# A new order for the written list of attention and early routing steps in a fused attention and expert kernel

## The chip, the cores and the metric

The kernel runs on one core of a Trainium2 chip. The metric is device time in microseconds (us). The engines are named as in the profile: PE (TensorE), DVE (VectorE), ACT (ScalarE), POOL (GpSimd), and SP (SyncE), which issues most DMAs.

## The reference

```
x = attention(q, k, v)             # 2 batches, 8 heads, 576 tokens, head_dim 64, window of 64 tokens
x = x as [1152 tokens, 512]
x = moe(x): expert = argmax(x @ w_gate), gate = softmax at it, at most cap = 288 tokens per expert
            out[token] = gate * (relu(x[token] @ w1[expert]) @ w2[expert])     # 8 experts, 512 -> 1024 -> 512
out = (g @ w_out), h = x @ w_in, g = h * clip(h + 3, 0, 6) / 6                # 512 -> 2048 -> 512
```

## The kernel before

**Stages.** Attention works on nine tiles of 128 tokens (index j) and on 18 halves of heads (index g, two for each j). The routing of the first five tiles ("early routing") runs inside attention's tail: it picks the expert with the most tokens among them, gathers up to 128 of that expert's rows from DRAM, and runs that expert on them with weights loaded ahead ("early loads", eight of 512 KB into the tile `early`). Then come the other experts and the dense layer. Their order is set by a planner with costs and due times that starts from the state in which attention ends.

**The list.** Attention and early routing are not planned at build time. They are written as one list of words, `ATTENTION` (L317), which `run_nodes` (L434) walks: each word is a step, a number behind the point is its tile or half, and `:a` or `:v` puts a copy on ACT or DVE. Every engine takes its own steps in the list's order and waits by semaphores for what a step needs, so the list is an order for each engine and not a timetable between them. The words that matter here:

- `lq lk lv`: loads of 256 KB of q, k, v by SP; `st.j`: store of tile j's attention output to `x_dram`, also by SP.
- `tq tk tv`, `pt`, `tw`: transposes on PE; `eq ek ev`, `ep`, `ew`, `ex`: the copies of these out of PSUM, on ACT or DVE (`ep.16` is a copy into the tile pT, `ex.8` two copies into vx and vy); `cv0 cv1 cv2`: copies of v on POOL.
- `s.j`: scores on PE (L574); `m.g`: mask and maximum on DVE (L587, four scans and their sums); `e.g`: exponentials on ACT (L600); `av.j`: values on PE (L628); `f.j`: division and logits on DVE (L640).
- `top pl fl gE ie`: early routing on DVE (L130 to L795); `pl` writes the expert's number to `eI` (L746), `ie` writes the row numbers and `sgE`, the gates. `pp`, `ix`: its counts and indices on PE. `hotp`: products for the later routing on POOL (L892).
- `wl.u.h`: an early load by SP (L271 for w1, L274 for w2); it needs `eI`. `ga`: the gather of the early expert's rows from `x_dram` into the tile c, issued by POOL (L800); it needs `ie` and the stores of tiles 0 to 4.
- `sE`: scaling of the gathered rows by their gates on ACT (L468); `tE`: their transposes on PE (L815); `xE`: copy of these into `early` on ACT; `e0.u` to `e3.u`, `er`, `et`, `eh`: the early expert on its first three units.
- `ch cn pL rk sa px sx g0 ...`: the routing of all tiles, up to the first gather for the other experts, into `first_w`.

**PSUM banks.** `gw`, `tw`, `pp`, `ix` and `tE` share one bank, the tag "x" (L100), so `tE` can be written only when the copies `ex.8` of `tw.8` have been read out of it.

**SP.** All DMAs of SP go out in order. A store that waits for its tile holds back every load behind it. The DMAs of SP and those of POOL are different queues on the same DMA engines.

```
node("ga", {"P": 0.4}, early_gather, ["ie"], lag=6.0)
node("sE", {"A": 0.61, "V": 0.5}, early_scale, ["ga"])
node(("wl", u, h), {"D": 1.46}, early_load(u, h), ["pl"], lag=2.3)
```

Of the kernel before, what the change touches and what calls it, by code (L numbers as in the profile page):

```python
# [23 lines left out]
def tile_kernel(ctx, tc, q, k, v, w_gate, w1, w2, w_in, w_out, out, cap):  # L24
# [87 lines left out]
    ex = const.tile(T3, F32, name="ex")  # L112
# [175 lines left out]
    def big(name, dt=F32):  # L288
        return rt.tile([128, NJ, E], dt, name=name)

    def sq(name):
# [7 lines left out]
    p1, bT, rk = logits, ex, big("rk")  # L299
    sa = rt.tile([128, NJ], F32, name="sa")  # L300
# [14 lines left out]

    NWARM = 9
    ATTENTION = """  # L317
        lq.0 tq.0 lk.0 tk.0 lk.1 eq.0:a lq.1 lq.2 ek.0:a tk.1 s.0 lv.0 m.0 tq.1 ek.1:a tq.2 eq.1:a m.1 e.0 wg tv.0
        s.1 eq.2:v pt.0 ev.0:v e.1 ep.0:a gw.0 ew.0:a lk.2 m.3 m.2 tk.2 pt.1 ek.2:a ep.1:v rc tw.0 lv.1 lq.3 lk.3
        cv1.0 tv.1 e.2 s.2 pt.2 ev.1:a lv.2 lk.4 tq.3 ex.0:v cv1.1 cv2.1 cv0.1 e.3 tk.3 eq.3:a cv0.0 ek.3:a av.0 m.5  # L320
        m.4 f.0 gw.1 ep.2:a s.3 e.4 m.7 cv2.0 ew.1:a pt.3 lq.4 ep.3:a tw.1 ex.1:v m.6 tv.2 tk.4 ev.2:a e.5 lv.3 pt.4
        ek.4:a ep.4:v tq.4 eq.4:v cv0.2 av.1 gw.2 f.1 e.6 lv.4 s.4 e.7 pt.6 cv0.3 tv.4 ew.2:v tv.3 cv1.2 tw.2 cv2.3
        ep.6:v lq.5 pt.5 ev.4:a lk.5 tk.5 ev.3:a cv2.2 cv1.3 ep.5:a tq.5 pt.7 ex.2:v ek.5:a eq.5:a av.2 gw.3 lq.8
        lk.6 m.8 m.9 ep.7:v cv1.4 s.5 cv0.4 tk.6 cv2.4 e.9 ew.3:a f.2 m.11 tw.3 lq.6 lv.6 lq.7 tq.6 e.8 ex.3:a pt.9
        gw.4 m.10 st.0 eq.6:a ep.9:v ew.4:v av.3 tw.4 cv0.6 pt.8 e.11 ek.6:a lv.5 lk.7 s.6 ex.4:a cv0.5 f.3 ep.8:a
        av.4 e.10 tk.7 tv.6 cv2.5 m.12 ek.7:a pt.10 ev.6:a tq.7 ep.10:a f.4 top gw.6 cv1.5 tq.8 m.13 ew.6:a eq.7:a
        lv.8 pp tv.5 eq.8:a cv2.6 ev.5:a pt.11 lk.8 cv1.6 lv.7 e.13 s.7 pl gw.5 st.4 tv.8 fl st.2 cv0.7 st.3 ew.5:a
        ep.11:a st.1 tw.5 gE ex.5:a pt.13 cv1.7 tw.6 av.5 e.12 ex.6:a m.14 tv.7 ix ev.8:a ep.13:a ev.7:a tk.8 ie
        ek.8:a cv0.8 pt.12 wl.2.1 gw.7 ep.12:a wl.3.1 ew.7:a m.15 f.5 wl.0.0 tw.7 cv1.8 wl.2.0 s.8 wl.1.0 e.15 pt.15
        e.14 ga hotp.3 ep.15:a wl.1.1 hotp.0 st.5 wl.0.1 wl.3.0 ex.7:v m.17 e.17 av.6 m.16 gw.8 pt.14 ew.8:a f.6  # L330
        pt.17 ep.14:a tw.8 av.7 e.16 ep.17:v pt.16 ex.8:a f.7 sE:a ep.16:a tE st.7 st.6 xE:a cv2.7 av.8 f.8 e0.1 ch
        e1.1 e0.0 pL er.1:v hotp.1 hotp.2 hotp.4 cn rk e1.0 sa hot.6 et.1 er.0:a et.0 eh.1:a e0.2 hot.8 hot.7 eh.0:a
        e2.0 px e1.2 sx e3.0 gt g0 hot.5 e2.1 gc pg e3.1 er.2:v sg
    """
    with ExitStack() as actx:
        ac = actx.enter_context(tc.tile_pool(name="ac", bufs=1))
# [379 lines left out]
        e1 = [ac.tile([128, 1], F32, name=f"e1_{i}") for i in range(2)]  # L716
        et = [ac.tile([128, NE], F32, name=f"et_{i}") for i in range(5)]
# [332 lines left out]
    for n, (small, b) in enumerate(TEAMS):  # L1050
        at_ = dict.fromkeys("abw", 0)
        order = ORDER[n]
        for c in order:
            f = at_[c]
# [867 lines left out]
    for g, (small, b) in enumerate(TEAMS):  # L1922
        st = start[False, small[0]]
# [81 lines left out]
    for n, (rest, u) in enumerate(own):  # L2005
        r = own_hidden(rest, u, r_up)
        if rest and u < 3:
            s, i, _ = rows_at[u]
# [83 lines left out]
```

## Time and profile before

| | |
|---|---|
| median of 3 runs | 412.59 us (412.42 to 412.99) |
| the profiled execution | 413.24 us |
| its span, first to last instruction | 411.5 us |
| mean granted TensorE clock | 0.994 |
| PE busy | 398.0 us (97%) |
| DVE, ACT, POOL busy | 277.5, 236.0, 49.7 us |
| moved by DMA | 65.43 MB, mean 159 GB/s |

Times in the rows count from the span's first instruction. A row of a timeline is the start, the duration, the engine, the line of the kernel, the operation, and what it writes and reads; in square brackets stands how long the engine was idle before it and what ended that. PE's matmuls overlap, so its busy time is not the same as its peak. SP's DMA issues are short; the transfers behind them are not.

### The profile page before, as it was taken

What the parts mean: (1) busy time and instruction counts of PE and PEld (TensorE: products, weight loads), DVE (VectorE), ACT (ScalarE), POOL (GpSimd) and SP (SyncE); (2) the same over time, 40 slices, a digit from 0 to 9 for tenths busy, and PEclk for the clock granted to TensorE, in tenths of its full rate; (3) what the DMA queues carried; (4) which work ended last, traced back from release to release, by engine and by line L of the source; (5) the groups of instructions that cost most, each with busy time, mean ns of one, the idle gap of its engine ahead of it and who ended that gap; (6) DMA issues with size and microseconds to landing.
All of it is one profiled execution on the core that took longest, in us unless ns stands there. A gap on an engine that the chain in (4) does not pass through costs nothing.

```text
span 411.5 us, 8431 instructions
## 1 busy us (share of the span) xinstructions
PE 398.0 (97%) x3066; PEld 341.2 (83%) x3066; DVE 277.5 (67%) x772; ACT 236.0 (57%) x519; POOL 49.7 (12%) x109
## 2 busy tenths in 40 slices
PE   8999989999999999999999999999999999999992
PEld 4888676669998999798899898888888888989981
DVE  1898956898789789866798999368794222222530
ACT  3898961876776566657877575466672223232320
POOL 8443414040011000000000000000000000200211
PEclk9999999999999999999999999999999999999997
DMA  9996986996687989999500740041500000100101
GB/s 171 207 211 156 300 305 203 364 299 210 214 283 248 358 278 298 312 353 308 211 2 0 245 165 2 1 133 73 205 1 2 0 0 2 76 27 0 51 30 56
DMA packets 63842, 65.43 MB, mean 159 GB/s; under 512 B 30688, under 2 KB 47072, under 8 KB 63792
## 3 DMA queue, kind: packets, MB, share of 16 engines
q1 hardware_dynamic: 62224, 59.79, 46.8%
q0 software_dynamic: 1568, 5.01, 3.7%
q8 instruction: 26, 0.43, 0.4%
q14 instruction: 24, 0.20, 0.1%
HBM read 60.08 MB, written 4.72 MB: 157 GB/s over the span
## 4 chain that ended last, share of the span: by engine, by line
PE 89%; DMA 3%; DVE 3%; ACT 2%; issue 1%; POOL 0%; POOLq 0%; ACTq 0%; DVEq 0%
PE banks L244 75%; PE banks L510 2%; DMA c<-x_dram,eI 2%; PE banks L574 2%; PE banks L628 2%; PE banks L610 1%; PE banks L1473 1%; PE banks L667 1%; PE banks L1498 1%; DMA out_dram<-part,cidx 1%; PE banks L1308 1%; PE banks L1557 1%; DMA x_dram<-xt 1%; PE banks L1406 0%; PE banks L540 0%
## 5 line engine op out<-in xcount | busy, mean ns | idle before, releaser
L244 PE MATMUL banks<-x,wt 128*128 128x320 f32 (+3 forms) x432 | 79.8, 336 | 0.0
L244 PEld LDWEIGHTS banks<-x,wt 128*128 128x128 f32 x432 | 70.8, 188 | 7.1
L244 PE MATMUL banks<-wt,g 128*128 128x512 f32 x288 | 69.6, 390 | 0.0
L263 DVE TENSOR_TENSOR wt<-raw,wt 128x512 fp32r<-128x512 f32 x100 | 64.5, 686 | 4.6 <-ACT wt L258 4.3
L1619 DVE SCALAR_TENSOR_TENSOR gf<-r,banks 128x320 f32<-128x320 f32 (+3 forms) x48 | 26.5, 553 | 60.2 <-ACT r L1616 60.1
L1616 ACT ACTIVATE r<-banks,c_three 128x320 f32<-128x320 f32 (+3 forms) x48 | 27.9, 582 | 68.3 <-PE banks L244 68.1
L244 PEld LDWEIGHTS banks<-wt,g 128*128 128x128 f32 x288 | 53.7, 188 | 10.6
L258 ACT CAST wt<-raw 128x512 fp32r<-128x512 f32 x100 | 58.9, 630 | 4.6 <-PE banks L244 4.0
L244 PE MATMUL banks<-xT,wt 128*128 128x224 f32 (+2 forms) x288 | 38.2, 282 | 0.0
L244 PE MATMUL banks<-h,wt 128*128 128x224 f32 (+2 forms) x288 | 37.0, 279 | 0.0
L244 PEld LDWEIGHTS banks<-xT,wt 128*128 128x128 f32 x288 | 34.8, 191 | 1.6 <-issue 0.4
L244 PEld LDWEIGHTS banks<-h,wt 128*128 128x128 f32 x288 | 34.6, 192 | 0.8 <-issue 0.8
L1622 ACT CAST g<-gf 128x320 fp32r<-128x320 f32 (+2 forms) x40 | 21.4, 534 | 16.5 <-DVE gf L1619 16.4
L1625 DVE TENSOR_TENSOR g<-gf,g 128x320 fp32r<-128x320 f32 (+2 forms) x40 | 23.4, 584 | 10.1 <-ACT g L1622 9.4
L1662 POOL DMA_INDIRECT out_dram<-raw,cidx x4 | 3.9, 983 | 203.9 <-ACT raw L1659 196.4
L244 PE MATMUL banks<-x,wt_fixed 128*128 128x320 f32 (+3 forms) x144 | 26.8, 337 | 0.4 <-ACT x L1389 0.4
L244 PEld LDWEIGHTS banks<-x,wt_fixed 128*128 128x128 f32 x144 | 23.5, 188 | 3.0 <-ACT x L1389 0.7
L206 ACT ACTIVATE c<-raw 128x512 f32<-128x512 f32 x32 | 21.6, 674 | 6.2 <-DVE raw L229 4.6
L244 PE MATMUL banks<-wt_fixed,g 128*128 128x512 f32 x96 | 23.2, 390 | 0.0
L600 ACT ACTIVATE pe<-neg,nmx 128x128 f32<-128x128 f32 x72 | 22.7, 400 | 0.0
L222 DVE SCALAR_TENSOR_TENSOR c<-raw,c 128x512 uint32<-128x512 uint32 x32 | 22.1, 690 | 0.7
L587 DVE CUSTOM_DVE_ANT_0 neg<-banks,tmask 128x128 f32<-128x128 f32 x72 | 16.1, 286 | 8.5 <-PE banks L574 8.3
(310 smaller groups left out, 627.5 us busy)
## 6 DMA issues: line engine op xcount, KB each, us to landing
raw<-in_moe_w_dram SPq DMA_DIRECT2D x56, 512.0 KB, 5.3
raw<-in_moe_w_in_dram SPq DMA_DIRECT2D x16, 512.0 KB, 6.0
raw<-in_moe_w_out_dram SPq DMA_DIRECT2D x16, 512.0 KB, 6.1
early<-in_moe_w_dram SPq DMA_DIRECT2D x8, 512.0 KB, 7.2
x_dram<-xt SPq DMA_DIRECT2D x9, 256.0 KB, 5.1
q_sb<-in_q_dram SPq DMA_DIRECT2D x8, 256.0 KB, 4.9
k_sb<-in_k_dram SPq DMA_DIRECT2D x8, 256.0 KB, 4.6
v_sb<-in_v_dram SPq DMA_DIRECT2D x8, 256.0 KB, 5.5
```

What stands on the lines that cost most here:

```text
L206: nc.scalar.activation(box["c"].bitcast(F32), box["hi"].bitcast(F32), AF.Abs)
L222: nc.vector.scalar_tensor_tensor(out=box["c"], in0=box["hi"], scalar=0xC0000000, in1=box["c"], op0=ALU.bitwise_and, op1=ALU.bitwise_or,)
L244: nc.tensor.matmul(out, l, r, start=(start and n == 0), stop=(stop and n == len(pairs) - 1))
L258: nc.scalar.copy(hi, r)
L263: V.tensor_tensor(out=lo, in0=r, in1=hi.bitcast(F32), op=ALU.subtract)
L510: nc.tensor.transpose(pt[:, hp, :], t[:, 2 * hp : 2 * hp + 2, :].rearrange("p h d -> p (h d)"), ident)
L587: V.tensor_tensor_reduce(out=neg[:, hp, :], in0=box["sp", g][:, hp, :], in1=tmask[:, first, :], scale=-1.0, scalar=3.0e38, op0=ALU.add, op ...
L600: nc.scalar.activation(pe[:, hp, :], neg[:, hp, :], AF.Exp, bias=nmx[:, hp : hp + 1], scale=-1.0)
L1616: nc.scalar.activation(r, ph, AF.Relu, bias=c_three)
L1619: V.scalar_tensor_tensor(out=gf, in0=r, scalar=6.0, in1=ph, op0=ALU.min, op1=ALU.mult)
L1622: nc.scalar.copy(hi, gf)
L1625: V.tensor_tensor(out=lo, in0=gf, in1=hi.bitcast(F32), op=ALU.subtract)
```

## The change

The list `ATTENTION` is replaced by another order of the same 309 words. The words were searched anew on a replay of the list in which a gather lands behind the loads that are queued ahead of it. 27 of the copies change between ACT and DVE. No other line of the kernel changes.

```diff
     ATTENTION = """
-        lq.0 tq.0 lk.0 tk.0 lk.1 eq.0:a lq.1 lq.2 ek.0:a tk.1 s.0 lv.0 m.0 tq.1 ek.1:a tq.2 eq.1:a m.1 e.0 wg tv.0
...
+        lq.0 tq.0 eq.0:v lk.0 lv.0 cv1.0 tk.0 cv0.0 tv.0 ev.0:a lk.1 lq.1 lk.2 wg ek.0:v s.0 tk.1 tq.1 m.1 ek.1:a
...
```

**SP around the early loads.** These are SP's instructions from the fourth early load's number on; DMAs into `early` are the early loads, the DMA into `x_dram` is the store of a tile, and the rows with ISA set an address. Before:

```order
L271 ISA
L271 DMA early_107<-in_moe_w1_dram 128x4x256
L271 ISA
L271 DMA early_107<-in_moe_w1_dram 128x4x256
L274 ISA
L274 DMA early_107<-in_moe_w2_dram 128x2x512
L660 DMA x_dram_80<-xt_1153 128x512
L274 ISA
L274 DMA early_107<-in_moe_w2_dram 128x2x512
L271 ISA
L271 DMA early_107<-in_moe_w1_dram 128x4x256
```

Of the change, from the same count of instructions:

```order
L274 ISA
L274 DMA early_107<-in_moe_w2_dram 128x2x512
L271 ISA
L271 DMA early_107<-in_moe_w1_dram 128x4x256
L274 ISA
L274 DMA early_107<-in_moe_w2_dram 128x2x512
L274 ISA
L274 DMA early_107<-in_moe_w2_dram 128x2x512
L660 DMA x_dram_80<-xt_1258 128x512
L271 ISA
L271 DMA early_107<-in_moe_w1_dram 128x4x256
```

Eight early loads go out in both. Two of them stood behind the store of tile 5; now one stands behind the store of tile 6, and seven ahead of it.

**DVE between the expert's number and the gather's index.** The rows are those at the end of `fl` (L156, L750) and the beginning of `gE` (L771, L159); L587 is one mask step, `m.14`.

```order
 L156 SCALAR_TENSOR_TENSOR sb<-q_91,pos 128x5
 L750 TENSOR_SCALAR A1E<-c_i128h,et_217 128x128 x2
+L587 ISA neg,nmx<-banks,tmask 128x128
+L587 ISA nmx 128x1
+L587 ISA neg,nmx<-banks,tmask 128x128
+L587 ISA nmx 128x1
+L587 ISA neg,nmx<-banks,tmask 128x128
+L587 ISA nmx 128x1
+L587 ISA neg,nmx<-banks,tmask 128x128
+L587 ISA nmx 128x1
 L771 TENSOR_REDUCE et_220<-ex 128x5
 L159 TENSOR_SCALAR A_93<-c_i128h,sb 128x128
```

A mask step stands now between `fl` and `gE`. Between `gE` and `ie` one stood before (`m.14`) and one stands now (`m.15`).

**ACT around the scaling of the gathered rows.** L468 on the tile c64 is `sE`, the copies into vx and vy are `ex.8`, the one into pT is `ep.16`, the one into `early` is `xE`. Before:

```order
L600 ACTIVATE pe_1278<-neg_1231,nmx_1232 128x128 x4
L466 COPY vx2_187<-banks_84 128x8x8
L466 COPY vy2_190<-banks_84 64x8x8
L468 ACTIVATE c64_1191<-c64_1191,sgE_133 128x512
L466 COPY pT_1300<-banks_84 128x512
L466 COPY early_107<-banks_84 128x512
```

Of the change:

```order
L600 ACTIVATE pe_1240<-neg_1218,nmx_1219 128x128 x4
L468 ACTIVATE c64_1155<-c64_1155,sgE_133 128x512
L466 COPY vx2_187<-banks_84 128x8x8
L466 COPY vy2_190<-banks_84 64x8x8
L466 COPY pT_1301<-banks_84 128x512
L466 COPY early_107<-banks_84 128x512
```

The two copies of `ex.8` stood ahead of the scaling and stand behind it now.

## Rows read from the trace of the kernel before

**Rows 1.** Page part 4: the chain that ended last, shares of the span by engine.
```profile
PE 89%; DMA 3%; DVE 3%; ACT 2%; issue 1%; POOL 0%; POOLq 0%; ACTq 0%; DVEq 0%
```

**Rows 2.** Stretches: length, busy us of PE, PEld, DVE, ACT, POOL, granted clock, DMA.
```profile
5.20:37.00 31.80, 31.14 (x548) 26.20 (x547) 24.00 (x144) 26.87 (x78) 17.13 (x58) 1.00 1.02 202
37.00:56.25 19.25, 16.94 (x275) 13.25 (x275) 17.61 (x113) 17.30 (x53) 6.22 (x10) 1.00 0.85 281
56.25:204.90 148.65, 147.64 (x1231) 127.16 (x1231) 118.72 (x295) 98.94 (x223) 13.50 (x15) 1.00 0.85 281
204.90:400.00 195.10, 195.07 (x992) 170.71 (x993) 115.99 (x218) 91.62 (x166) 6.84 (x7) 1.00 0.15 53
```

**Rows 3.** The chain in order of time, 35 to 63 us: start, us, what.
```profile
35.70 1.23 PE banks L628 x32
...
42.04 0.05 DVE eI L746
...
47.38 8.07 DMA c<-x_dram,eI
...
60.65 2.13 DMA x_dram<-xt
```

**Rows 4.** ScalarE in order of time, 53 to 57 us.
```profile
54.27 0.20 ACT L466 COPY vx<-banks 128x64 f32<-128x64 f32 x1
54.37 0.21 ACT L466 COPY vy<-banks 64x64 f32<-64x64 f32 x1
55.48 0.72 ACT L468 ACTIVATE c<-c,sgE 128x512 f32<-128x512 f32 x1 [0.90 <-DMA c<-x_dram,eI]
56.10 0.57 ACT L466 COPY pT<-banks 128x512 f32<-128x512 f32 x1
```

**Rows 5.** PE's instructions in order of time, 54 to 57 us, idle before each.
```profile
54.48 0.66 PE L610 MATMUL banks<-ident,pe 128*128 128x128 f32 x4
56.25 0.66 PE L815 MATMUL banks<-ident,c 128*128 128x128 f32 x4 [1.12 <-ACT c L468]
56.84 0.28 PE L628 MATMUL banks<-vy,pT 128*64 128x73 f32 x1
```

**Rows 6.** SP's DMA issues in order of time, 43 to 50 us.
```profile
43.40 1.00 SPq L274 DMA_DIRECT2D early<-in_moe_w_dram  x2
44.60 1.63 SPq L271 DMA_DIRECT2D early<-in_moe_w_dram  x3
46.42 0.41 SPq L274 DMA_DIRECT2D early<-in_moe_w_dram  x1
49.38 0.34 SPq L660 DMA_DIRECT2D x_dram<-xt  x1
```

**Rows 7.** One stretch, columns as in the second group.
```profile
46.00:55.00 9.00, 7.98 (x143) 6.33 (x143) 7.93 (x52) 8.52 (x27) 2.69 (x5) 1.00 1.05 365
```

**Rows 8.** PE in order of time, at 10 us.
```profile
10.28 0.63 PE L510 MATMUL banks<-ident,v_sb 128*128 128x128 f32 x4 [0.33 <-ACT qd L468]
```

**Rows 9.** VectorE in order of time: one mask step's first scan and what follows it.
```profile
46.10 0.28 DVE L587 CUSTOM_DVE_ANT_0 neg<-banks,tmask 128x128 f32<-128x128 f32 x1
...
46.94 0.15 DVE L793 CAST eI<-banks 128x1 int32<-128x1 f32 x1
```

**Rows 10.** GpSimd in order of time, 47 to 67 us.
```profile
48.61 0.76 POOL L892 TENSOR_TENSOR A1t<-A,c_tok 128x128 f16<-128x128 f16 x2
...
65.74 1.00 POOL L800 DMA_INDIRECT first_w<-x_dram,sidx  x1 [8.32 <-DVE gate L965]
```

**Rows 11.** VectorE in order of time: the first use of first_w's gathered rows.
```profile
69.32 0.49 DVE L1300 TENSOR_SCALAR first_w<-first_w,sgate 128x512 f32<-128x512 f32 x1 [0.74 <-DMA first_w<-x_dram,sidx]
```

**Rows 12.** The early loads' tile: from issue to landing.
```profile
DMA to landing us min/median/max: 3.9/7.2/9.2
```

**Rows 13.** The chain in order of time, 69 to 71 us.
```profile
69.31 1.73 PE banks L244 x8
```

## What was predicted before the changed kernel ran

> **What bounds the kernel now.** I read the chain that ended last by engine first: 89% of the span is TensorE (PE) and 3% is DMA [rows 1]. Then the stretches: from 56.25 to 204.9 us PE is busy 147.64 of 148.65 us, and from 204.9 to 400 us 195.07 of 195.10 [rows 2]. So what follows 56.25 us is PE work in a fixed order, and a shift of its beginning reaches the end nearly whole. Before that, PE stands idle 0.66 us between 5.2 and 37 us and 2.31 us between 37 and 56.25 us [rows 2]. These 2.97 us are all that a better order of the list could take out of PE's own waits.
>
> Next, the chain in order of time around 56 us [rows 3]. It leaves PE after the fifth `av` (35.70 us), runs through VectorE's routing steps (`eI`, the expert's number, at 42.04) and then 8.07 us through the gather of the early expert's rows (`c<-x_dram,eI`, 47.38 to 55.45). ScalarE scales these rows at 55.48, having waited for that DMA [rows 4], and PE turns them at 56.25 (step tE). PE's own rows say the same: its last work ahead of tE starts at 54.48 and takes 0.66 us, and 1.12 us pass idle before tE; av.8 follows at 56.84 [rows 5]. The end of this kernel therefore hangs on when the gather lands. The reader is to see that the gather has two neighbours: SP issued six of the eight early loads of 512 KB from 43.40 to 46.83, all before the gather's issue at 47.38; the other two stand behind the store that began at 49.38 [rows 6]; the engines moved 365 GB/s from 46 to 55 us at a full share [rows 7].
>
> **The change, part by part.** Only the list is different; PE has the same steps ahead of tE in both lists, only in another order, and behind the early expert's steps the order of every engine is the same as before; among these, halves of units 0 to 2 trade places, which changes no amount of work.
>
> (a) *The first 37 us.* Both lists do the same 51 steps of PE up to av.4, and the DMAs up to there are loads of q, k and v at 202 GB/s and a full share [rows 2]. PE idles 0.66 us here, so the new order can give at most 0.66 us. It can lose where a load that moved back is needed early: v.0 goes ahead of k.1 and k.2, but the sixth load is again the one whose turn comes at about 10.3 us (tk.2 now, tv.0 before, 0.33 us idle, put down to a copy on ScalarE [rows 8]). I take 0, with -0.6 and +0.5 as bounds; the loss is bounded by the price of one load of 256 KB less than half waited for, 256 KB at 202 GB/s = 1.3 us.
>
> (b) *VectorE between eI and the gather.* Before, one mask step (a row of four L587 scans and their sums) stood between the expert's steps and the gather's index; now two stand there. One such step takes 46.94 - 46.10 = 0.84 us [rows 9]. Behind it on VectorE wait the gates, the index, and through them the gather on POOL: issue at 47.38 + 0.84 = 48.22. The product hotp.0 that now stands ahead of the gather on POOL (0.38 us, half of the 0.76 of a pair [rows 10]) runs while POOL waits for the index, and costs nothing; without that cover it would cost 0.38.
>
> (c) *The loads ahead of the gather.* SP waits for eI alone before the first early load; it does not wait for the list's place of the gather. In the new list seven loads stand ahead of the store that waits (x_dram<-xt), six before. At 0.61 us from issue to issue (44.60 to 46.42 for three [rows 6]) the seventh leaves at 43.40 + 6 x 0.61 = 47.06, ahead of the gather's 48.22. What one load more costs the gather no row shows directly. Below: nothing but the 0.84 us of (b), if the 8.07 us hold from its issue. Middle: it lands one load later, 512 KB / 365 GB/s = 1.44 us [rows 7]. Above: both, 2.28 us. For the middle speaks that an unhindered gather is much shorter: first_w's is issued at 65.74 and its rows are used at 69.32, 3.58 us later [rows 10, 11]; so 8.07 - 3.58 = 4.5 us of the 8.07 are the queue, three loads of 1.44, and a later issue is absorbed by a queue that is full anyway. I take 1.44.
>
> The Trainium skill, "DMA: Bandwidth & Descriptors", section "Queues, rings and completion order", speaks against it: each engine goes round-robin between the rings it has work for, packet by packet, so the gather's ring would not stand behind SP's at all. By that one more queued load would cost nothing and the sum would hold only (b) and (d). The 4.5 us above do not agree with an even share, which would add about the gather's own 256 KB, 0.7 us at that rate; the measured rows decide.
>
> (d) *ScalarE behind the gather.* The two copies of ex.8 (0.20 and 0.21 us, 54.27 to 54.58 [rows 4]) ran before the scaling of the gathered rows; now they stand behind it. They read the one PSUM bank that tE writes, so tE waits for them. From the landing to av.8 it was 56.84 - 55.48 = 1.36 us. Now: scaling 56.10 - 55.48 = 0.62, copies 0.31, some 0.05 to PE, tE 56.84 - 56.25 = 0.59: 1.57. The other way, through ep.16, is 0.62 + 0.31 + 0.57 = 1.50 and does not decide. Cost 0.21 us.
>
> (e) *What goes out later.* The eighth early load now waits for store 6, that is for f.6 at about 53 us. It took at most 9.2 us to land before [rows 12], so 62.4 us; it is needed at 69.31, the first matmuls of the fourth unit [rows 13]. Cover 6.9 us. Store 7 is queued behind store 8: store 8 lands 2.13 us after 60.65 [rows 3], store 7 some 0.4 later, 63.2, and the gather that needs both starts at 65.74 [rows 10]. Cover 2.5 us. Both sides of these move with the shift. I cost them at nothing.
>
> *Sum:* 0 + 1.44 + 0.21 = +1.65 us. The profiled execution took 413.24 us (span 411.5 and 1.74 around it) and would take 414.9; the median of the runs is 412.59, 0.65 lower than that execution, so the forecast is 414.2.
>
> **Rivals.**
> - *The gather's time holds from its issue*, because the queue delays it by a fixed depth or shares with it from some point on, whatever else is queued. Then only 0.84 + 0.21 = 1.05 us are lost: 413.6. For it: the gather's 8.07 us are one measurement, and six loads were queued before it while it may have been held by the first few of them. Against: the 4.5 us of queue above. The round-robin of the Trainium skill's page, named in (c), would have this outcome.
> - *Later issue and one more load add up:* 0.84 + 1.44 + 0.21 = 2.49 us, 415.1. Needs a gather that queues behind what is there when it is issued and no load served meanwhile; but 0.84 us of queue is served meanwhile.
> - *The other side: the gather lands early.* In the list three loads now stand ahead of it, five before. If SP's loads came at the list's pace, the gather would land at least 2 x 1.44 us sooner, by about 52.6; then PE's last work (54.48 + 0.66) and its copy (0.57) decide, av.8 starts at about 55.9 in place of 56.84, and the time is 411.6. It decides as soon as the gather lands before 56.84 - 1.57 = 55.27. Against: SP's six loads had gone out by 46.83 with five of them ahead of the gather in the list [rows 6], so SP runs ahead of the list.
> - *Nothing that can be measured:* the first part gives its 0.6 us and the gather's lateness is at its lower bound, 1.05: +0.45; 413.0.
>
> **How the numbers follow.** Forecast (one load more, 414.2): 0.45. Time from the issue (413.6): 0.20. Both add (415.1): 0.10. Early gather (411.6): 0.13. No difference (413.0): 0.12. About 0.2%, 0.8 us, is what a measurement of this kernel can tell from no change, so slower begins at 413.4. Slower is then 0.45 + 0.10 and most of 0.20, less the tail where the first part gives back 0.6 us: 0.70. Same takes the rest of these and the 0.12: 0.17. Faster 0.13. The range leaves out the early gather and takes in the no-difference case and both costs at once: 412.8 to 415.2. The forecast's own range is 413.6 to 414.9.
>
> **What would show it.** (b): the gather's issue on POOL near 48.2, with eI still near 42. (c): seven early loads on SP before that issue and none held; the gather landing near 56.9. (d): ScalarE's copies behind the scaling, PE idle about 2.8 us before tE (1.12 before), av.8 near 58.5. After that every row 1.6 us later. It is wrong if the first part moves eI by more than half a microsecond either way, if the gather lands by 55.3, or if the wait before tE is long enough for PE's granted clock to fall: in these rows it stayed at 1.00 through the longest wait before 400 us, 1.12 us, and a wait of 2.8 us no row shows.

## The result and the profile after

The changed kernel took 414.85 us (median of 21 executions, 412.97 to 416.83), the kernel before 412.54 us beside it (21 executions, 411.84 to 413.62). The ratio is 1.0051, 95% interval 1.0038 to 1.0064: 1.6 to 2.6 us slower. The profiled execution took 414.76 us with a span of 413.1, 1.52 us more than the profiled one of before. The forecast was 414.2, in a range of 412.8 to 415.2.

The sign is the one forecast, and the time lies in the range, 0.65 us above the forecast. The trace shows other causes for it. First, the stretches of the changed kernel; columns as in [rows 2], the granted clock is the third number from the end.

```profile
5.20:37.00 31.80, 30.94 (x550) 26.16 (x549) 25.70 (x140) 27.82 (x87) 16.73 (x57) 1.00 1.05 210
37.00:56.25 19.25, 16.00 (x274) 13.02 (x272) 17.25 (x110) 16.61 (x53) 7.74 (x14) 1.00 0.83 275
57.40:60.70 3.30, 3.30 (x32) 2.83 (x27) 1.48 (x8) 1.26 (x6) 0.00 (x0) 0.50 0.31 112
60.70:204.90 144.20, 143.57 (x1184) 123.77 (x1183) 116.66 (x287) 95.63 (x213) 12.29 (x12) 1.00 0.86 284
204.90:400.00 195.10, 194.70 (x995) 170.28 (x994) 115.73 (x219) 93.22 (x169) 6.86 (x7) 1.00 0.15 53
```

The third line has no counterpart before: from 57.4 to 60.7 us PE is busy all the time, at a granted clock of 0.50, the lower of its two levels (1.2 GHz). In finer slices the clock falls at 57.36 and is back at 60.75, so 3.4 us at half speed, which is 1.7 us of lost work. Next the chain in order of time, as in [rows 3].

```profile
48.22 7.19 DMA c<-x_dram,eI
...
55.43 0.72 ACT c L468
...
56.41 0.66 PE banks L815 x4
57.07 1.87 PE banks L628 x32
58.94 3.71 PE banks L244 x12
```

The gather was issued at 48.22, 0.84 later than in [rows 3], as step (b) had it. GpSimd's row and SP's issues, in order of time as in [rows 6, 10], show it behind seven loads, the last two of which share a row (45.92 and 47.07), and all of them ahead of the store at 52.40.

```profile
48.22 1.19 POOL L800 DMA_INDIRECT c<-x_dram,eI  x1 [1.57 <-DVE sgE L795]
```
```profile
45.92 1.52 SPq L274 DMA_DIRECT2D early<-in_moe_w_dram  x2
52.40 0.34 SPq L660 DMA_DIRECT2D x_dram<-xt  x1
```

But it landed at 55.41 in place of 55.45, not at 56.9: the 8.07 us became 7.19 in this execution. ScalarE and PE around it, in order of time, answer to [rows 4, 5].

```profile
55.43 0.72 ACT L468 ACTIVATE c<-c,sgE 128x512 f32<-128x512 f32 x1 [2.07 <-DMA c<-x_dram,eI]
56.06 0.20 ACT L466 COPY vx<-banks 128x64 f32<-128x64 f32 x1
56.15 0.21 ACT L466 COPY vy<-banks 64x64 f32<-64x64 f32 x1
56.26 0.58 ACT L466 COPY pT<-banks 128x512 f32<-128x512 f32 x1
```
```profile
53.77 0.60 PE L610 MATMUL banks<-ident,pe 128*128 128x128 f32 x4
56.41 0.66 PE L815 MATMUL banks<-ident,c 128*128 128x128 f32 x4 [2.04 <-ACT vy L466]
57.00 0.28 PE L628 MATMUL banks<-vy,pT 128*64 128x73 f32 x1
```

The copies of ex.8 stand behind the scaling, and tE starts 1.00 us after the landing (0.80 before), step (d). PE's own last work before tE starts 0.71 us earlier than before (53.77 against 54.48) and ends at 54.37 instead of 55.14, so its wait grew from 1.12 to 2.04 us although tE is only 0.16 us later. The clock falls 0.95 us after that wait ends. av.8 starts 0.16 us later than before and the span is 1.6 us longer, which the 1.7 us of the clock cover.

### The profile page after: what moved, and what is told of

Read it like the earlier page. It is cut to its first block, busy times and chain, and to the rows that moved or that the text cites. A ratio compares the mean times of both kernels' runs of the same rounds, so it can differ in the third digit from the quotient of the medians.

```text
span 413.1 us, 8437 instructions
## 1 busy us (share of the span) xinstructions
PE 398.5 (96%) x3066; PEld 342.3 (83%) x3066; DVE 278.9 (68%) x765; ACT 235.4 (57%) x526; POOL 49.6 (12%) x109
## 4 chain that ended last, share of the span: by engine, by line
PE 88%; DMA 4%; DVE 3%; ACT 1%; SPq 1%; issue 1%; POOL 0%; POOLq 0%; ACTq 0%; DVEq 0%
PE banks L244 76%; PE banks L628 2%; DMA c<-x_dram,eI 2%; PE banks L510 2%; PE banks L574 2%; DMA k_sb<-in_k_dram 1%; PE banks L610 1%; PE banks L1473 1%; SPq L478 1%; PE banks L1498 1%; DMA out_dram<-part,cidx 1%; PE banks L1308 1%; PE banks L1557 1%; DVE neg L587 1%; PE banks L1406 0%
## 5 line engine op out<-in xcount | busy, mean ns | idle before, releaser
L209 ACT ACTIVATE raw<-raw 128x512 uint32<-128x512 uint32 x32 | 21.5, 673 | 0.0
```

The source lines that it names most:

```text
L209: nc.scalar.activation(box["lo"], box["lo"], AF.Copy, scale=2.0 ** -29)
```

## Experiments

Twelve kernels were timed or profiled, in three groups on three chips (e1 to e4, e5 to e8, e9 to e12); the kernel before ran beside each group (medians 412.81, 413.12 and 413.10 us). Where a text below speaks of the clock held or fallen in an execution, it goes by the mean granted clock of the whole execution: 0.993 or more, or 0.992 or less. This parts the executions of the changed kernel cleanly (413.81 us and less, 414.52 and more), but it is a rough sign elsewhere: in the third group an execution of the kernel before that took 412.82 us counts as fallen. Times without a trace behind them are medians.

| run | median us | ratio to before, 95% interval | clock fallen |
|---|---|---|---|
| changed kernel | 414.85 | 1.0051 (1.0038 to 1.0064) | 14 of 21 |
| e1: clock held by extra matmuls | 413.84 | 1.0026 (1.0017 to 1.0035) | 0 of 12 |
| e2: three loads ahead | 411.74 | 0.9977 (0.9967 to 0.9987) | 0 of 12 |
| e3: m.14 alone moved back | 414.19 | 1.0035 (1.0019 to 1.0050) | 7 of 12 |
| e4: before, seven loads | 413.11 | 1.0000 (0.9984 to 1.0017) | 0 of 11 |
| e5: before, late issue | 413.81 | 1.0009 (0.9986 to 1.0031) | 3 of 12 |
| e6: six loads, clock held | 413.79 | 1.0005 (0.9988 to 1.0022) | 0 of 12 |
| e7: early issue, clock held | 412.73 | 0.9980 (0.9963 to 0.9997) | 0 of 12 |
| e8: before, three loads | 412.11 | 0.9971 (0.9953 to 0.9990) | 0 of 12 |
| e9: three loads, early issue | 411.79 | 0.9970 (0.9956 to 0.9983) | 0 of 12 |
| e12: (b) and (d) undone | 412.71 | 0.9998 (0.9976 to 1.0020) | 2 of 12 |

e10 and e11 had one execution each, for the trace (412.65 and 413.03 us). In the kernel before the clock fell in 1 of 35, 5 of 35 and 4 of 23 executions beside these groups.

### The clock held (e1)

```diff
-        ... hotp.1 ex.8:a pt.16 ep.16:a tE wl.2.1 st.6 ...
+        ... hotp.1 ex.8:a pt.16 ep.16:a fill tE wl.2.1 st.6 ...
+        node("fill", {"PE": 0.0}, lambda e: [nc.tensor.matmul(t, warm[:, 0:128], warm, start=True, stop=True) for t in [bank("s")] * 6])
```

> The changed kernel with six matmuls of 512 columns on a tile of zeros, into a free PSUM bank, between PE's last attention step (pt.16) and tE, where PE waited 2.04 us. They compute nothing that is used. Theory 1 (the loss is the granted clock, 0.50 to 0.67 from 57 to 60.6 us, and the clock fell because PE stood idle): the wait is cut to under 1 us, the clock stays at 1.00 until 400 us, tE still starts near 56.4, and the time falls by about 1.6 us, from 414.85 to 413.2, with a spread between runs as small as that of the kernel before. Theory 2 (the clock's fall is incidental, the work behind tE is late because of the gather and the copies): nothing changes, 414.8.

Theory 1 holds. PE in order of time and, below it, the chain, with the same order of work as in the changed kernel:

```profile
54.46 1.46 PE L884 MATMUL banks<-warm 128*128 128x512 bf16 x6
57.00 0.66 PE L815 MATMUL banks<-ident,c 128*128 128x128 f32 x4 [1.09 <-ACT vy L466]
```
```profile
57.66 1.18 PE banks L628 x32
58.84 2.79 PE banks L244 x12
```

The same two pieces took 1.87 and 3.71 us in the changed kernel: 0.69 + 0.92 = 1.61 us that only the clock explains. No execution lost the clock, where 14 of 21 had (and 7 of 12 in e3, on e1's chip); the ratio falls from 1.0051 to 1.0026, 0.25% or 1.03 us, about 1.6 us in two executions of three. The 21 executions of the changed kernel split the same way: 415.2 us where the clock fell, 413.5 in the seven where it held. But 413.84 is not 412.8: another 1.0 us is lost without the clock, and the gather of this trace landed at 56.0, issued at 48.22 as in the changed kernel.

### Loads ahead and issue taken apart (e3 to e7)

Step (c) by itself, on the kernel before (e4):

```diff
-        e.14 ga hotp.3 ep.15:a wl.1.1 hotp.0 st.5 wl.0.1 wl.3.0 ...
+        e.14 ga hotp.3 ep.15:a wl.1.1 hotp.0 wl.0.1 st.5 wl.3.0 ...
```

> The kernel before with the seventh early load moved ahead of store 5, so that seven are queued ahead of the gather, as in the changed kernel; nothing else. The prediction's step (c): the gather lands 1.44 us later, at 56.9, PE waits 2.6 us, and the time is 412.5 + 1.44 = 414.0, or 415.6 if the clock falls as well. The rival (a load more behind the fourth costs the gather nothing): it lands at 55.4, and the time is 412.5.

The time did not change (1.0000, at most 0.7 us more), which leaves no room for 1.44 us. The profiled execution (413.95 us) is the longest of the eleven: its gather's last packets were late (9.25 us from the issue), PE waited longer than in the changed kernel, and still the clock stayed, as PE's row and the stretch show:

```profile
57.00 0.66 PE L815 MATMUL banks<-ident,c 128*128 128x128 f32 x4 [2.31 <-ACT c L468]
```
```profile
57.40:60.70 3.30, 3.30 (x44) 2.85 (x43) 1.58 (x8) 1.68 (x8) 0.78 (x3) 1.00 0.50 182
```

Step (b) by itself, on the kernel before (e5):

```diff
-        e.14 ga hotp.3 ep.15:a wl.1.1 hotp.0 st.5 ...
+        e.14 hotp.3 hotp.0 hotp.1 hotp.2 hotp.4 ga ep.15:a wl.1.1 st.5 ...
```

> The kernel before with all five products hotp ahead of the gather on GpSimd (1.9 us of work from about 46.1 us on), so that the gather is issued some 0.8 us later, near 48.2, with the same six loads queued ahead of it: step (b) of the prediction by itself. Theory 1 (the queue sets the landing, a later issue is absorbed): no change, 412.8. Theory 2 (the gather takes a fixed time from its issue): 412.8 + 0.8 = 413.6.

The interval of the ratio alone holds both theories. Where the clock held, the nine executions have a median of 413.6 against 413.0 of the thirty of before, which is near theory 2's 0.8 us: it points at theory 2 and does not show it. In the trace the gather was issued at 48.81, later than meant (5.13 us behind the first early load, 3.98 before), and landed 7.44 us later.

The same two steps undone on the changed kernel with the matmuls of e1, six loads (e6) and the early issue (e7):

```diff
 e6
-        ... pt.16 ep.16:a fill tE wl.2.1 st.6 av.8 ...
+        ... pt.16 ep.16:a fill tE st.6 wl.2.1 av.8 ...
 e7
-        ... gw.6 ew.6:a m.14 av.5 tv.8 tw.6 cv2.7 gE pt.12 tv.7 e.14 ex.6:a cv0.6 m.15 ep.12:a ix ...
+        ... gw.6 ew.6:a av.5 tv.8 tw.6 cv2.7 gE m.14 pt.12 tv.7 ex.6:a cv0.6 m.15 ep.12:a e.14 ix ...
```

> The changed kernel with the six matmuls that hold the clock, and with store 6 ahead of the seventh early load, so that six loads are queued ahead of the gather as in the kernel before: step (c) undone, the clock held. To compare with the changed kernel with the matmuls alone (413.84). Theory 1 (the queue sets the landing): it lands 0.4 to 0.9 us earlier, 413.0 to 413.4. Theory 2 (the issue sets it): 413.8. The prediction's 1.44 us for the load: 412.4.

> The changed kernel with the six matmuls that hold the clock, and with m.14 behind the gates and e.14 behind ep.12 on ScalarE, so that the index does not wait for the copies behind e.14 as it did when m.14 alone was moved: the gather issued near 47.4 with seven loads ahead of it, step (b) undone. To compare with 413.84. Theory 1 (the queue sets the landing): 413.8. Theory 2 (the issue sets it): 0.8 us less, 413.0.

GpSimd's rows of e6 and of e7:

```profile
48.24 1.19 POOL L800 DMA_INDIRECT c<-x_dram,eI  x1 [1.46 <-DVE sgE L795]
```
```profile
47.75 1.19 POOL L800 DMA_INDIRECT c<-x_dram,eI  x1 [0.99 <-DVE sgE L795]
```

Six loads in place of seven: 413.79, where seven took 413.84 on another chip. The ratios of the two in the table lie further apart (1.0005 and 1.0026, 0.9 us). Set against the executions of the kernel before whose clock held on the same chip (412.96 and 412.80), e6 is 0.83 us slower and e1 1.04, so 0.2 us is left for the seventh load. The issue at 47.75: 412.73, 1.06 us less than e6 on the same chip (the slowest execution of e7 took 413.35 us, the fastest of e6 413.13). In the traces the gather of e7 lands 0.67 us earlier than that of e6 (55.33, 56.00) and tE starts 0.68 us earlier (56.33, 57.01). The issue counts, and the seventh load costs at most half of its 1.44 us (0.7 us by e4's interval). Before this, m.14 alone had been moved behind the gates (e3):

```diff
-        ... gw.6 ew.6:a m.14 av.5 tv.8 tw.6 cv2.7 gE pt.12 ...
+        ... gw.6 ew.6:a av.5 tv.8 tw.6 cv2.7 gE m.14 pt.12 ...
```

> The changed kernel with the mask step m.14 behind the gates (gE) again, as before the change; nothing else. The gather is issued at 47.4 in place of 48.2. Theory 1 (the landing is set by the loads queued, not by the issue): it lands at 55.4 all the same, PE waits 1.5 to 2 us for it, and the time is 413.0 (clock held, since the exponentials of half 14 and PE's work on them come later and shorten the wait) to 414.8 (clock fallen). Theory 2 (7.2 us from the issue): it lands at 54.6, the clock stays, and the time is 412.4.

It tells nothing on the landing, since the gather wasn't issued earlier but at 48.61. PE's row says why:

```profile
47.78 0.26 PE L789 MATMUL banks<-rhsE,A1E 128*128 128x3 f16 x5 [1.30 <-ACT vy L466]
```

The index needs the shared bank, which the copies of ex.6 still held; on ScalarE these stood behind the exponentials of half 14, and they behind m.14. So e7 moved e.14 as well.

### How much of the queue a gather waits for (e2, e8, e10, e11)

Three loads on the changed list (e2) and on the list before (e8); e10 and e11 are e8 with one and two loads more ahead of store 5. The other loads stand behind it, and are left out of the diff where their old words go.

```diff
 e2
-        ek.7:a wl.0.1 wl.2.0 fl ...  hotp.0 ie wl.0.0 ev.7:a f.5 ga hotp.2 ...
+        ek.7:a wl.0.0 wl.1.0 wl.2.0 fl ...  hotp.0 ie ev.7:a f.5 st.5 wl.0.1 wl.1.1 wl.2.1 wl.3.0 wl.3.1 ga hotp.2 ...
 e8
-        pt.12 wl.2.1 gw.7 ep.12:a wl.3.1 ew.7:a m.15 f.5 wl.0.0 tw.7 cv1.8 wl.2.0 s.8 wl.1.0 e.15 ...
+        pt.12 wl.0.0 gw.7 ep.12:a wl.1.0 ew.7:a m.15 f.5 wl.2.0 tw.7 cv1.8 st.5 s.8 wl.0.1 e.15 ...
```

> The changed kernel with three early loads (the first halves of units 0 to 2) ahead of the gather instead of seven: store 5 stands behind the third load and holds the other five back until about 49.5 us. Theory 1 (the gather is served about when the fourth load queued ahead of it has ended, and what is queued behind does not matter): with three it lands by about 52 us, PE does not wait for it any more, the clock stays at 1.00, and the time is 411.5 to 412.0, below both kernels. Theory 2 (the gather takes some 7 to 8 us from its issue whatever is queued): it lands at 55.4 again, and the time is 414.8. Theory 3 (each load queued ahead costs the gather 1.44 us, as the prediction had it): four fewer, 49.7 us at the earliest, bounded by its own 3.6 us at 51.8; the time as in theory 1.

> The kernel before with three early loads (the first halves of units 0 to 2) ahead of the gather, store 5 behind the third and the other five loads behind store 5. The gather lands by about 52 us, tE waits for PE's own work (55.14) and the scaling, av.8 starts near 55.9 in place of 56.84: about 0.9 us less than before, 411.9. If another wait takes the place of this one (the loads that go out late are needed, store 6 or 7 is late), no change, 412.8.

> The kernel before with four early loads ahead of the gather, store 5 behind the fourth. Read from the trace: the time from the end of the gather's issue to its first packet, which was 0.7 us with three loads and 3.5 to 3.7 us with six and seven. Theory 1 (the gather waits for the loads that the DMA engines have already taken in, and these are at most about 3.6 us of work): with four it waits for the rest of them, 2.2 to 3.1 us, and lands at 53 to 54. Theory 2 (the wait is 3.6 us whenever loads are still queued at all): 3.6. The prediction's theory (one load, 1.44 us): 0.7 + 1.44 = 2.1, and no end to it with more loads.

> The kernel before with five early loads ahead of the gather, store 5 behind the fifth. Theory 1 (at most some 3.6 us of work is taken in ahead): first packet 3.5 to 3.7 us after the issue's end, as with six and seven. The prediction's theory: 1.44 us more than with four and 1.44 us less than with six.

The gather's own packets are those of the queue software_dynamic. The DMA view of a stretch counts the packets, MB and share of each queue. Here is, for four kernels, the stretch from the end of the gather's issue on GpSimd to just ahead of its first packet; no row of software_dynamic is in any of them. Kernel before (48.57 to 52.20 us), changed kernel (49.41 to 52.90), five loads (48.55 to 51.80), four loads (48.30 to 50.50):

```profile
q1 hardware_dynamic: 1319, 1.32, 108.6%
```
```profile
q1 hardware_dynamic: 911, 1.26, 103.4%
```
```profile
q1 hardware_dynamic: 796, 1.20, 103.0%
```
```profile
q1 hardware_dynamic: 640, 0.78, 103.4%
```

With four loads 0.78 MB go first, what was left of the four. With five it is 1.20 MB, again nearly what was left of them; with six it is 1.32 and with seven 1.26 MB, about two and a half loads of 0.52 MB, although more stood in SP's queue. The amount goes by the end of the gather's issue and not by the place of a load in the queue: counted from the first early load's issue, SP's queue had moved 2.57 MB when the first packet came in the kernel before (43.40 to 52.25 us) and 3.07 MB in e3 (43.06 to 53.28), whose gather was issued 1.23 us later. From the end of the issue to the first packet:

| loads ahead of the gather | not yet landed at the issue's end | first packet, us later |
|---|---|---|
| three (e2, e8, e9) | 2 (e8: two loads; e2 and e9: a load and store 5) | 0.70, 0.72, 0.71 |
| four (e10) | 3 | 2.28 |
| five (e11) | 4 | 3.33 |
| six (before, e5, e6) | 5, 5 (with store 5), 4 | 3.70, 3.65, 3.53 |
| seven (changed, e1, e3, e4, e7, e12) | 5, 5, 5, 6, 5, 5 | 3.52, 3.45, 3.51, 3.65, 3.50, 3.48 |

That is theory 1 of e10 and e11: the wait grows with the loads up to about 3.6 us and no further. The 2.28 us of four loads alone would fit the prediction's 2.1 as well; but at 1.44 us a load six would take about 5 us, and six take 3.53 to 3.70, seven 3.45 to 3.65. With no load ahead of it the gather of first_w in the kernel before needs as long as with three: its issue ends at 66.74, no packet of any queue moves until 67.4, and its first one comes at 67.43, 0.69 us later. All loads here are of one size and move at 356 to 371 GB/s in these stretches, so the runs can't tell whether the bound is one of bytes, of transfers or of time, nor what holds it. With three loads SP's and ScalarE's rows of e8 read:

```profile
43.34 1.57 SPq L271 DMA_DIRECT2D early<-in_moe_w_dram  x3
49.33 0.34 SPq L660 DMA_DIRECT2D x_dram<-xt  x1
49.86 2.34 SPq L274 DMA_DIRECT2D early<-in_moe_w_dram  x3
```
```profile
54.38 0.72 ACT L468 ACTIVATE c<-c,sgE 128x512 f32<-128x512 f32 x1
```

The gather, issued at 47.32, lands at 51.77, ahead of the scaling's turn on ScalarE at 54.38. In e2 and e8 it is off the chain, and both are faster than the kernel before (0.9977 and 0.9971).

### The two remaining moves, and the best of the lists (e12, e9)

e12 is e7 without the matmuls, with ex.8 ahead of the scaling:

```diff
-        ... av.7 sE:a ew.8:v ep.17:v cv1.8 tw.8 f.7 hotp.1 ex.8:a pt.16 ...
+        ... av.7 ew.8:v ep.17:v cv1.8 tw.8 f.7 hotp.1 ex.8:a sE:a pt.16 ...
```

> The changed kernel with its steps (b) and (d) undone and nothing else: m.14 behind the gates, e.14 behind ep.12, and ex.8 ahead of the scaling. Seven loads stay ahead of the gather, and no matmuls are added. If the loss is (b), (d) and the clock that falls in the wait they make, the gather is issued near 47.7, PE waits about 1.4 us, the clock holds in nearly all runs, and the time is that of the kernel before, within 0.3 us. If the seventh load costs its 1.44 us, it is 1.4 us slower than before.

The changed kernel's loss is gone (0.9998, and the interval ends at 1.0020, below the 1.0038 at which that of the loss begins), with its seven loads and every other part of the change in place. PE's wait and tE:

```profile
55.64 0.66 PE L815 MATMUL banks<-ident,c 128*128 128x128 f32 x4 [0.86 <-ACT c L468]
```

The clock still fell in 2 of 12. e9 is e2 with the moves of e7 (no matmuls, ex.8 left behind the scaling):

> The changed kernel with three early loads ahead of the gather (as in the run with three loads) and with m.14 behind the gates and e.14 behind ep.12 (as in the run with the early issue), without extra matmuls. PE's waits for the index (0.66 us) and for the late gather are both gone: 411.3 to 411.5, the fastest so far. If PE only waits elsewhere instead (pt.12 and what follows come later, since the exponentials of half 14 do), it equals the run with three loads, 1.0 us below the kernel before.

411.79 us, 0.30% faster than the kernel before (0.17% to 0.44%) and ahead of both kernels; against e2 and e8 no difference can be told. It did not come to the 411.5 hoped for, though the kernel before was slower on this chip (413.10) than beside the changed kernel (412.54). PE waits for ScalarE alone, which scales as soon as its own exponentials are done, with no wait for the gather. ScalarE's and PE's rows:

```profile
53.98 0.71 ACT L468 ACTIVATE c<-c,sgE 128x512 f32<-128x512 f32 x1
```
```profile
54.95 0.66 PE L815 MATMUL banks<-ident,c 128*128 128x128 f32 x4 [0.18 <-ACT vy L466]
```

## Why the number was right and its main reason was not

**(a)** held: PE idles 0.86 us in the first 37 us (0.66 before), inside the bounds. eI came 0.1 us earlier (41.83 in VectorE's order, 41.94 before).

**(b)** was sized right, 0.84 us, and the issue stands where it was put, at 48.22 (from eI on it is 0.95 us later, and eI itself 0.11 earlier). Its effect was misjudged: the prediction let it be "absorbed by a queue that is full anyway". e7 against e6 (1.06 us less for an issue 0.49 us earlier in the two traces) shows that a later issue is paid, and e5 points the same way (0.7 us more, where the clock held, for an issue 1.15 us later behind the first early load). The exact share is open: the landing scatters by more than the 0.84 (7.11 to 9.25 us from the issue with five or more loads ahead of the gather, by the last packets).

**(c)** is the step that failed: 1.44 us for one load more. It read some three loads' work of queue out of 4.5 us (by e8's 4.44 us from issue to landing, with two loads not landed, it is 3.6 us, two and a half loads), which is near, but it took it that the gather lands one load later for each load more that is queued. It stands behind a bounded amount, 1.2 to 1.3 MB, that five loads already fill. The nine first packets behind six and seven loads, 3.45 to 3.70 us after the issue's end, show no price of the seventh; in the times e4 leaves it at most 0.7 us, and e6 against e1 0.2. What the runs show is the rival "the gather's time holds from its issue", for which the prediction gave "a fixed depth" as one reason, with its 1.05 us: the changed kernel takes 413.5 where the clock held, 1.0 us more than the kernel before beside it, and e1 413.84, 1.0 us more as well. The round-robin between rings that the Trainium skill, "DMA: Bandwidth & Descriptors", section "Queues, rings and completion order", states would give the same for the seventh load; by it alone, though, the first packet would not wait behind SP's loads either, and here it does, 3.3 to 3.7 us in ten traces. The measurement decides: a bounded amount of SP's loads goes first.

**(d)** was right: from landing to tE it is 1.0 us in the traces of the changed kernel, e1 and e3, and 0.80 in those of before and e4, so 0.2 us.

**(e)** was right: no wait of PE for the loads and stores that go out later has a price that shows. The one wait that PE's rows mark between 57.5 and 110 us is 0.26 us, in the changed kernel as in e2, e8 and e9 with five loads behind store 5.

**What the sum left out** is the clock: 1.7 us in two executions of three, some 1.1 us of the mean. The prediction named it as what would make it wrong and put no price on it. It had the wait ahead of tE grow to 2.8 us by a late gather; it grew to 2.04, most of it because PE's last work ended 0.77 us earlier, which no step had. So 0.84 + 0.2 + 1.1 = 2.1 us, the measured loss (2.1 by the ratio, 2.3 by the medians), came out near 1.44 + 0.21 by luck: two errors nearly cancel, 1.44 for the seventh load and nothing for the clock and the issue. e1 takes the clock's part away and leaves 1.0 us; e12 undoes the issue and the copies, shortens the wait with them, and takes away the whole.

What stays open: which waits make the clock fall. It fell after 2.04 us (changed) and 1.94 us (e3), and not after 2.31 us (e4), 1.88 us (e5) and 1.12 us (before, in that trace). The length of PE's wait alone does not decide it, and why e4 kept it in all eleven executions while the changed kernel lost it in 14 of 21 was not settled.

## What to carry to other kernels

A gather issued behind large loads waits for a bounded part of them: here two transfers not yet landed at the end of its issue did not delay its first packet, a third delayed it by 1.6 us, a fourth by another 1.0, and further ones by 0.4 us at most. So either few loads go out ahead of it and the rest are held behind a store, or its issue time is what counts, and work ahead of its index is moved behind. A wait of PE in front of dense work has two prices, its length and, in some executions, 1.7 us of half clock behind it: look at the granted clock right behind the wait, and for clusters that far apart among the executions.

## What the runs showed of the hardware that was not expected

- From the end of the gather's issue to its first packet, with five or more loads ahead of it, the transfers queued by SP moved 1.20 to 1.32 MB over 3.3 to 3.7 us, whether five, six or seven loads were queued and whether the issue began at 46.95 or 48.81 us. With three ahead the first packet came 0.70 to 0.72 us after the issue's end, and 0.69 us for a gather with nothing ahead.
- The gather's last packets came much later than most of them: in e4 fifteen of the sixteen engines had finished it by 54.7 us and the last at 56.2. One trace's landing is therefore no measure of a change of a microsecond; the first packet repeated within 0.25 us.
- The granted clock fell to 0.50 for 3.4 us in the trace of the changed kernel and in that of e3 (57.49 to 60.90), 0.95 and 0.36 us after PE had resumed work and while it was fully busy.
